# Transposes as pairs of 64-row products, and a first block whose exchanged input is made by copies

## The chip, the core and the metric

The kernel runs on one core of a Trainium2 chip. The metric is the device time of one execution in microseconds (us). The core has a matrix engine (TensorE; in the rows PE for its products and PEld for the loads of their stationary operand), a vector engine (VectorE, DVE), a scalar engine (ScalarE, ACT), GpSimd (POOL) and SyncE (SP), which issues the DMA transfers.

## What is computed

Three stages follow each other, in float32: a convolution whose seven weights per token and head come out of a softmax, and two feed-forward layers.

```python
w = softmax(weight_gen)                        # 2 x 4096 tokens, 8 heads, 7 taps
out[b, s, h] = sum over k of w[b, s, h, k] * x[b, s + k - 6, h]   # x: 2 x 4096 x 192
h = out @ w_in                                 # 192 -> 2048
y = (h * np.cos(h)) @ w_out                    # 2048 -> 192
h2 = y @ w_in2
result = np.maximum(0.01 * h2, h2) @ w_out2
```

## The kernel before

The 8192 tokens are cut into 16 blocks of 512. A block is first convolved with the tokens on the partitions (VectorE, or in parts GpSimd), then turned, so that the 192 channels lie on the partitions and the 512 tokens along them, then taken through the first layer (m = 0) and the second (m = 1), and turned back for the output. A layer is worked in 16 chunks of 128 hidden channels. For accuracy every operand is split into a high and a low float32r part, and a product is made as high x high, high x low and low x high.

**Products as pairs of 64 rows.** The 192 channels are 128 + 64, so products with 128 rows would leave half of the array empty on the rest. All products of the layers have 64 rows (`SIDES` are the lower and the upper 64 partitions), and two of them, one on each side, run in the array at the same time (lines 789 and 799; the rows say `64*128 64x512`). Since a side can only read its own 64 partitions, each block's input stands in three tiles: `x..n` (channels 0 to 127, high and low), `x..s` (the same with its halves exchanged, made by two DMAs in `crossed`, line 473), and `x..r` (the last 64 channels on both sides). An input piece (`hidden`, line 786) is nine products: three with `n`, three with `r`, three with `s`.

**Transposes.** A transpose is a product with the identity. In `attention` (14 blocks) the op `both` makes four of 128 x 128 out of `xa` (line 561) and two out of `xb` (line 566), into the PSUM banks `tm` and `tr`. In `attention_summed` (the two blocks that run first, `LINE[:2]` = 2 and 3) the seven taps are transposed one by one and added in PSUM (line 599). In `take` each finished block of the second layer is turned back in the same way (lines 908 and 912). All of these use 128 rows. In what follows one such group of six in the middle of the products is called a turn: there are 14 of the convolution and 16 of the output. `keep_going` (line 936) are idle transposes that keep the engine running at the start.

**Evacuation.** `turned` copies `tm` to `x0n` high (ACT) and subtracts for the low part (DVE). `place` does the same for the rest, 64 x 256 on each side, and sends the other side's half by one DMA per side; `place_whole` does it without a DMA for the two first blocks. 

**What sets the order.** The function is run once on a plan: each step is an `op` with a due time, a cost for each engine that may do it, what it reads and writes, and its buffers. `Plan.emit` is a list scheduler: it writes the engines' instruction streams from these due times and costs. On the chip each instruction waits by semaphores for what it reads itself; the plan's dependencies only decide where in its engine's stream it stands. `piece` makes the ops of the products and `part` cuts the list of steps into pieces; an input piece there reads all of `n`, `s` and `r` at once (line 804).

Of the kernel before, what the change touches and what calls it, by code (L numbers as in the profile page):

```python
# [14 lines left out]
ALU = mybir.AluOpType  # L15
# [184 lines left out]
def conv_attention_moe_moe(ctx, tc, x, weight_gen, w_in1, w_out1, w_in2, w_out2, out):  # L200
# [27 lines left out]
    SWITCH = 0.43  # L228
# [68 lines left out]

    def minus(e, out, a, b):
        eng[e].tensor_tensor(out=out, in0=a, in1=b.bitcast(F32), op=ALU.subtract)  # L299
# [173 lines left out]
    def crossed(m, b, due):  # L473
        xn, xs, xr = x_of[m, b]
        for j in range(2):
            to, of_ = SIDES[j], SIDES[1 - j]
            op(due, {"SP": 0.8}, lambda e, to=to, of_=of_: nc.sync.dma_start(
                out=xs()[to].bitcast(F32), in_=xn()[of_].bitcast(F32)), [("xhi", m, b), ("xlo", m, b)], [("xs", m, b, j)], [xn, xs])

    def attention(b, begins):  # L480
# [76 lines left out]
        tm, tr = bank(f"tm{b}", ("tq", 2)), bank(f"tr{b}", ("tq", 2))  # L557
# [10 lines left out]
        def both(e):  # L568
            turn(e)
            turn_rest(e)  # L570

        op(last, {"PE": 0.66 + SWITCH}, both, [(k, b, q) for q in kinds for k in ("xam", "xbr")] + ["ident"],
           [("tm", b), ("tr", b)], [xa, xb, tm, tr])
        turned(b, last, tm, tr)

    def attention_summed(b, begins):

        xt, own = xt_of[b]
        ksm, smw, s0 = sm_of[b]
        tm, tr = bank(f"tm{b}", ("tq", 2)), bank(f"tr{b}", ("tq", 2))  # L580
        x_tiles(0, b)
        last = begins - 2
        for i, k in enumerate(reversed(range(K))):
            pr = row(f"pr{b}_{k}")
            reads = [ksm, ("xt", b, 1)]
            if k < HALO and b in LINE[:2]:
                reads.append(("xt", b, 2))
            if k < own:
                reads += [("xt", b, 0, *j) for j in ((0,), (1,), ("z", 0), ("z", 1))]

            def product(e, k=k, pr=pr):
                win = xt().rearrange("p (q h g) -> p q h g", h=H, g=G)[:, k : k + Q]
# [3 lines left out]
            def total(e, to, c, i=i, pr=pr):  # L596
                for q in range(Q):
                    v = pr()[:, q, c]
                    nc.tensor.matmul(  # L599
                        to()[: v.shape[-1], q * P : (q + 1) * P], v, ident, is_transpose=True,  # L600
                        start=i == 0 and q == 0, stop=i == K - 1 and q == Q - 1,
                    )
# [3 lines left out]
            for to, key, c, late in ((tm, "tm", slice(0, P), 0.5), (tr, "tr", slice(P, D), 0.55)):  # L606
                op(due + late, {"PE": 0.44}, lambda e, to=to, c=c, total=total: total(e, to, c),
                   [("pr", b, k), "ident"] + ([(key, b)] if i else []), [(key, b)], [pr, to])
        turned(b, last, tm, tr)

    def turned(b, last, tm, tr):
        xn, xs, xr = x_of[0, b]
        op(last + 0.4, {"ACT": 0.59}, lambda e: copy(e, xn()[:, 0], tm()), [("tm", b)], [("xhi", 0, b)], [xn, tm])
        op(last + 0.8, {"DVE": 0.68}, lambda e: minus(e, xn()[:, 1], tm(), xn()[:, 0]), [("tm", b), ("xhi", 0, b)], [("xlo", 0, b)], [xn, tm])
        crossed(0, b, last + 1)
        if b in SUMMED:
            place_whole(b, last + 0.6, tr)
            return
        place(0, b, last + 1, ("tr", b), tr, lambda: tr()[:, :HT])

    def place_whole(b, due, tr):

        xr = x_of[0, b][2]
        lo, up = SIDES
        op(due, {"ACT": 0.58}, lambda e: copy(e, xr()[lo, 0], tr()[lo]), [("tr", b)], [("rh", 0, b, 0)], [xr, tr])
        op(due + 0.2, {"DVE": 0.68}, lambda e: minus(e, xr()[lo, 1], tr()[lo], xr()[lo, 0]), [("tr", b), ("rh", 0, b, 0)], [("rl", 0, b, 0)], [xr, tr])
        op(due + 0.4, {"ACT": 0.58}, lambda e: copy(e, xr()[up, 0], tr()[lo]), [("tr", b)], [("rh", 0, b, 1)], [xr, tr])
        op(due + 0.6, {"DVE": (0.43,), "ACT": 0.63}, lambda e: copy(e, xr()[up, 1], xr()[lo, 1].bitcast(F32)), [("rl", 0, b, 0)], [("rl", 0, b, 1)], [xr])

    def place(m, b, due, key, src, v):  # L630

        xr = x_of[m, b][2]
        halves = (SIDES[0], slice(0, HT)), (SIDES[1], slice(HT, T))
        for i, (p, c) in enumerate(halves):
            op(due, {"ACT": 0.39}, lambda e, p=p, c=c: copy(e, xr()[p, 0, c], v()[p]), [key], [("rh", m, b, i)], [xr, src])
            op(due + 0.2, {"DVE": 0.42 if m == 0 else (0.41,)}, lambda e, p=p, c=c: minus(e, xr()[p, 1, c], v()[p], xr()[p, 0, c]),
               [key, ("rh", m, b, i)], [("rl", m, b, i)], [xr, src])
            op(due + 0.5, {"SP": 0.4}, lambda e, p=p, p2=SIDES[1 - i], c=c: nc.sync.dma_start(
                out=xr()[p2, :, c].bitcast(F32), in_=xr()[p, :, c].bitcast(F32)), [("rh", m, b, i), ("rl", m, b, i)], [("rx", m, b, i)], [xr])
# [136 lines left out]
    def chunk(pos, st, m, b, f):  # L776
# [27 lines left out]
        reads = [((n, "i", j), "hi", 0), ((n, "i", j), "lo", 0), ("xhi", m, b), ("xlo", m, b)]  # L804
        reads += [k for k in plan.writers if k[0] in ("xs", "rh", "rl", "rx") and k[1:3] == (m, b)]
# [3 lines left out]
        made["in", pos] = hidden, reads, [h, xn, xs, xr], kh  # L809
# [66 lines left out]
    def take(due, st, m, b, am, ar):  # L876
# [9 lines left out]
        halves = (slice(0, R), slice(0, HT), slice(R, P)), (slice(R, P), slice(HT, T), slice(0, R))  # L886
        op(due + 0.1, {"DVE": 0.68, "ACT": 0.58}, lambda e: copy(e, om(), am()), [k], [("om", m, b)], [am, om])
        for i, (p, c, p2) in enumerate(halves):
            op(due, {"ACT": 0.38}, lambda e, p=p, c=c, p2=p2: copy(e, sw()[p], ar()[p2, c]), [k], [("sw", m, b, i)], [ar, sw])
            op(due + 0.2, {"DVE": 0.42}, lambda e, p=p, c=c: nc.vector.tensor_tensor(  # L890
                out=s()[p], in0=ar()[p, c], in1=sw()[p], op=ALU.add), [k, ("sw", m, b, i)], [("s", m, b, i)], [ar, sw, s])
        if m == 0:
# [8 lines left out]
            place(1, b, due + 0.3, k, s, lambda: s())  # L901
            return
        o = row(f"osb{b}", "osb")
        pm, pr = bank(f"pm{b}", ("tq", 2)), bank(f"pr{b}", ("tq", 2))

        def main(e):
            for q in range(Q):
                nc.tensor.transpose(pm()[:, q * P : (q + 1) * P], om()[:, q * P : (q + 1) * P], ident)  # L908

        def rest(e):  # L910
            for j in range(2):
                nc.tensor.transpose(pr()[:, j * P : (j + 1) * P], s()[:, j * P : (j + 1) * P], ident)  # L912

        due += 5
        def both(e):
            main(e)
            rest(e)

        op(due, {"PE": 0.66 + SWITCH}, both, [("om", m, b), ("s", m, b, 0), ("s", m, b, 1)],
           [("pm", b), ("pr", b)], [om, s, pm, pr])  # L920
        op(due + 0.5, {"ACT": 0.59, "DVE": 0.69}, lambda e: copy(e, o()[:, :, :P], pm().rearrange("p (q t) -> p q t", q=Q)),
           [("pm", b)], [("osb", b, 0)], [pm, o])
        op(due + 0.6, {"ACT": 0.38, "DVE": 0.42}, lambda e: copy(
            e, o().rearrange("p (a j) d -> p j a d", a=2)[:, :, :, P:], pr()[:, :HT].rearrange("p (j a d) -> p j a d", j=2, a=2)),
           [("pr", b)], [("osb", b, 1)], [pr, o])
        op(due + 1, {"SP": 1.35}, lambda e: nc.sync.dma_start(out=of[:, Q * b : Q * b + Q, :], in_=o()),
           [("osb", b, 0), ("osb", b, 1)], [("out", b)], [o])
# [23 lines left out]
    def piece(key, nows, due):  # L951
        reads, writes, bufs, then = ["order"], ["order"], [], []
        for side, at in enumerate(key):
# [3 lines left out]
            if at[0] == "in":  # L957
                pos = 2 * at[1] + side
                _, r, bs, kh = made["in", pos]
                reads, bufs = reads + r, bufs + bs  # L960
# [40 lines left out]
    for key, nows in pieces:  # L1001
        dues = []
        for side, at in enumerate(key):
            if at:
                dues.append(2 * at[1] + side + (0 if at[0] == "in" else 2 * LAG + 1 + 0.3 * at[2]))
# [7 lines left out]
    for i in range(IDLE_TURNS):  # L1013
        op(3.0, {"PE": 0.44}, keep_going, [("tm", LINE[0]), ("tr", LINE[0])], (), [spare])
# [29 lines left out]
```

## Time and profile before

| | us |
|---|---|
| median of three runs (1210.36 to 1211.6) | 1211.28 |
| the profiled execution's own time | 1209.89 |
| its span (first to last instruction) | 1208.1 |

| engine | busy, us | share of the span |
|---|---|---|
| PE | 1182.8 | 98% |
| PEld | 1016.0 | 84% |
| DVE | 886.1 | 73% |
| ACT | 847.0 | 70% |
| POOL | 443.0 | 37% |

The span is shorter than the time by what lies around it, 1.79 us. Busy time of PE counts the two sides' products together where they overlap, and the ends of products are modelled; a busy PE is therefore read by the distance between the starts of products, not by its share. The granted clock is that of TensorE, 1.00 being 2.4 GHz and 0.50 being 1.2 GHz.

### The profile page before, as it was taken

The page shows a single profiled execution, that of the slowest core. Times are in us where ns is not written, and L with a number is a line of the kernel's source. Part 1 is how long each engine was busy: PE and PEld are TensorE (multiplying, and loading weights), DVE is VectorE, ACT ScalarE, POOL GpSimd, SP SyncE. Part 2 cuts the span into 40 slices and gives each one's busy share as a digit, 9 for nine tenths or more (in the row PEclk, how much of TensorE's full clock was granted, in tenths as well). Part 3 has the DMA queues.
Part 4 walks back from the last instruction along what each step waited for, and adds up shares of the span by engine and source line. Part 5 has one row for each costly group of instructions (what it writes and reads, how often), then busy time and mean ns, then how long its engine had stood idle before and what let it go on. Part 6 is the DMA issues. An engine that isn't in the chain of part 4 may idle for free.

```text
span 1208.1 us, 25074 instructions
## 1 busy us (share of the span) xinstructions
PE 1182.8 (98%) x10072; PEld 1016.0 (84%) x10072; DVE 886.1 (73%) x1299; ACT 847.0 (70%) x1484; POOL 443.0 (37%) x331
## 2 busy tenths in 40 slices
PE   7998899999999999999999999999999999999998
PEld 6786788888888888888888888888888888888886
DVE  6898887887868687786867768786776868746532
ACT  4898657886766767677676867767676676767753
POOL 4786632670523416052240614325051341504200
PEclk8999899999999999999999999999999999999999
DMA  7534320122120121211012120211212012020100
GB/s 195 162 80 112 106 75 14 40 60 53 47 53 1 47 53 63 53 46 46 10 47 53 47 53 10 77 30 47 53 47 53 1 47 53 14 54 14 28 1 27
DMA packets 30516, 62.69 MB, mean 52 GB/s; under 512 B 3396, under 2 KB 21314, under 8 KB 30400
## 3 DMA queue, kind: packets, MB, share of 16 engines
q1 hardware_dynamic: 30400, 61.08, 18.3%
q8 instruction: 80, 1.31, 0.5%
q14 instruction: 36, 0.29, 0.1%
HBM read 30.13 MB, written 6.29 MB: 30 GB/s over the span
## 4 chain that ended last, share of the span: by engine, by line
PE 92%; DMA 2%; DVE 2%; POOL 1%; issue 1%; ACT 1%; SPq 0%; DVEq 0%; POOLq 0%; ACTq 0%
PE ps L799 46%; PE ps L789 44%; PE ps L908 1%; DMA w01in<-in_moe_w_in 1%; PE ps L561 1%; PE ps L599 1%; DMA x1r<-x1r 1%; DMA xt<-in_x 0%; POOL ilo L299 0%; DMA x0s<-x0n 0%; PE ps L912 0%; DVE lo L299 0%; PE ps L566 0%; DVE g L828 0%; POOL w12in L725 0%
## 5 line engine op out<-in xcount | busy, mean ns | idle before, releaser
L299 POOL TENSOR_TENSOR lo<-g,hi 128x512 fp32r<-128x512 f32 x240 | 335.5, 1399 | 526.1 <-ACT hi L294 480.5
L799 PE MATMUL ps<-hi,ohi 64*128 64x512 f32 x1024 | 403.5, 394 | 0.0
L799 PE MATMUL ps<-hi,olo 64*128 64x512 f32 x1024 | 398.9, 390 | 2.7 <-POOL olo L299 2.7
L799 PE MATMUL ps<-lo,or 64*128 64x512 f32 x1024 | 399.6, 390 | 0.0
L799 PE MATMUL ps<-lo,ohi 64*128 64x512 f32 x1024 | 399.0, 390 | 0.1
L799 PE MATMUL ps<-hi,or 64*128 64x512 f32 x1024 | 398.5, 389 | 0.2 <-POOL or L299 0.2
L299 DVE TENSOR_TENSOR lo<-ps,hi 128x512 fp32r<-128x512 f32 x272 | 186.9, 690 | 162.9 <-ACT hi L294 156.8
L852 ACT ACTIVATE ps<-ps 128x512 f32<-128x512 f32 x256 | 148.8, 582 | 166.6 <-PE ps L789 132.6
L838 DVE TENSOR_TENSOR g<-ps,g 128x512 f32<-128x512 f32 x240 | 165.3, 689 | 86.1 <-ACT g L833 81.9
L799 PEld LDWEIGHTS ps<-hi,olo 64*128 64x128 f32 x1024 | 189.4, 185 | 18.9 <-POOL olo L299 3.1
L799 PEld LDWEIGHTS ps<-lo,ohi 64*128 64x128 f32 x1024 | 189.2, 185 | 16.4 <-DVE lo L299 0.5
L799 PEld LDWEIGHTS ps<-hi,ohi 64*128 64x128 f32 x1024 | 189.4, 185 | 16.1 <-issue 0.2
L799 PEld LDWEIGHTS ps<-lo,or 64*128 64x128 f32 x1024 | 189.5, 185 | 15.0 <-issue 2.4
L789 PE MATMUL ps<-x1n,ihi 64*128 64x512 f32 x512 | 199.6, 390 | 2.5 <-DVE x0n L299 2.5
L799 PEld LDWEIGHTS ps<-hi,or 64*128 64x128 f32 x1024 | 189.6, 185 | 13.4 <-POOL or L299 0.6
L789 PE MATMUL ps<-x0s,ihi 64*128 64x512 f32 x512 | 198.6, 391 | 1.8 <-DMA x0s<-x0n 1.8
L789 PE MATMUL ps<-x1r,ihi 64*128 64x512 f32 x512 | 199.8, 390 | 0.5 <-DMA x1r<-x1r 0.5
L789 PE MATMUL ps<-x1s,ihi 64*128 64x512 f32 x512 | 199.2, 389 | 0.7 <-DMA x1s<-x1n 0.7
L789 PE MATMUL ps<-x0n,ihi 64*128 64x512 f32 x512 | 199.6, 394 | 0.2 <-DVE g L838 0.2
L789 PE MATMUL ps<-x0r,ihi 64*128 64x512 f32 x512 | 198.0, 390 | 0.0
L833 ACT ACTIVATE g<-g 128x512 f32<-128x512 f32 x256 | 161.0, 631 | 45.3 <-DVE g L828 43.1
L828 DVE SCALAR_TENSOR_TENSOR g<-g,ps 128x512 f32<-128x512 int32 x256 | 174.7, 684 | 23.7 <-ACT g L821 18.8
(227 smaller groups left out, 2636.7 us busy)
## 6 DMA issues: line engine op xcount, KB each, us to landing
xt<-in_x SPq DMA_DIRECT2D x12, 960.0 KB, 5.4
x0s<-x0n SPq DMA_DIRECT2D x32, 256.0 KB, 3.8
x1s<-x1n SPq DMA_DIRECT2D x32, 256.0 KB, 3.7
out<-osb SPq DMA_DIRECT2D x16, 384.0 KB, 2.8
x0r<-x0r SPq DMA_DIRECT2D x28, 128.0 KB, 3.8
x1r<-x1r SPq DMA_DIRECT2D x28, 128.0 KB, 3.4
smw<-in_weight_gen SPq DMA_DIRECT2D x3, 448.0 KB, 4.9
xt<-in_x SPq DMA_DIRECT2D x3, 384.0 KB, 4.4
```

Of the source, the lines that this page charges most:

```text
L299: eng[e].tensor_tensor(out=out, in0=a, in1=b.bitcast(F32), op=ALU.subtract)
L561: nc.tensor.transpose(tm()[:, q * P : (q + 1) * P], xa()[:, q, :P], ident)
L599: nc.tensor.matmul(to()[: v.shape[-1], q * P : (q + 1) * P], v, ident, is_transpose=True, start=i == 0 and q == 0, stop=i == K - 1 and q = ...
L789: return nc.tensor.matmul(h(), w[rows, j, d], x()[rows, v], start=i == 0, stop=i == 8)
L799: return nc.tensor.matmul(to(), w[r, f % GF, :], v()[r], start=f == 0 and to_side == 0 and i in (0, 3), stop=f == NF - 1 and to_side == 1 ...
L828: nc.vector.scalar_tensor_tensor(out=g(), in0=g().bitcast(I32), scalar=-2 * math.pi, in1=h(), op0=ALU.mult, op1=ALU.add)
L833: nc.scalar.activation(out=g(), in_=g(), func=AF.Sin, bias=math.pi / 2)
L838: nc.vector.tensor_tensor(out=h() if bank_low else g(), in0=h(), in1=g(), op=ALU.mult)
L852: op(pos + 0.6, {"ACT": 0.58}, lambda e: nc.scalar.activation(out=h(), in_=h(), func=AF.Prelu, alpha=0.01), [kh], [kg], [h])
L908: nc.tensor.transpose(pm()[:, q * P : (q + 1) * P], om()[:, q * P : (q + 1) * P], ident)
```

## The change

Three things, beside the renaming that comes with them (`half`, `side_of`, `rows_of` only name slices).

1. All transposes that carry data become products of 64 rows: `turn64` takes one side's 64 partitions, with a 64 x 64 piece of the identity as the moving operand, and the two sides write two PSUM banks (`tx[0]`, `tx[1]`; `po[0]`, `po[1]` for the output). A turn is then 12 products where there were 6; a tap of a summed block is 16 where there were 8. What is copied out of PSUM is cut by bank, so that four copies of 128 x 256 and of 64 x 128 stand where one of 128 x 512 and one or two of 64 x 256 stood. `place` and `turned` send the second sides' halves in `second` as four DMAs, where there were two. The plan's cost of a turn loses `SWITCH` (0.43).
2. For the first block of the line (`LINE[0]`) `by_copies` makes `x0s` by four copies of 64 x 512 on DVE or ACT in place of two DMAs. The rest of the second summed block goes to its other side by one DMA in place of a copy.
3. In the plan an input piece is split in three (the products with `n`, with `r`, with `s`), and each reads only its own tiles. Seven idle transposes at the start read the new key.

```diff
+    def turn64(out, v, side, **flags):
+        r = SIDES[side]
+        nc.tensor.matmul(out, v, ident[r, r.start : r.stop], is_transpose=True, **{"start": True, "stop": True, **flags})
...
     def part(step):
         kind, p, i = step
-        return (kind, p) if kind == "in" else (kind, p, i // 3 if i < 6 else 2)
+        return kind, p, i // 3 if kind == "in" or i < 6 else 2
...
         def turn(e):
             for q in range(Q):
-                nc.tensor.transpose(tm()[:, q * P : (q + 1) * P], xa()[:, q, :P], ident)
-
-        def turn_rest(e):
+                for i in range(2):
+                    turn64(tx[i]()[:, q * R : (q + 1) * R], xa()[SIDES[i], q, :P], i)
             v = xb().rearrange("p j a r -> p j (a r)")
             for j in range(2):
-                nc.tensor.transpose(tr()[:, j * P : (j + 1) * P], v[:, j], ident)
...
+                for i in range(2):
+                    turn64(tx[i]()[:, HT + j * R : HT + (j + 1) * R], v[SIDES[i], j], i)
...
-        op(due, {"PE": 0.66 + SWITCH}, both, [("om", m, b), ("s", m, b, 0), ("s", m, b, 1)],
+        op(due, {"PE": 0.66}, back, [("om", m, b), ("s", m, b, 0), ("s", m, b, 1)], [("po", b)], [om, s, *po])
...
+        if b == LINE[0]:
+            by_copies(b, last + 0.9)
+        else:
+            crossed(0, b, last + 1)
...
+    def by_copies(b, due):
+        xn, xs, xr = x_of[0, b]
+        for v, k in enumerate(("xhi", "xlo")):
+            for j in range(2):
+                op(due + 0.4 * v, {"DVE": (0.43,), "ACT": 0.63}, lambda e, v=v, j=j: copy(e, xs()[SIDES[j], v], xn()[SIDES[1 - j], v].bitcast(F32)),
+                   [(k, 0, b, 0), (k, 0, b, 1)], [("xs", 0, b, j, v)], [xn, xs])
+
+    def second(m, b, due, keys):
+        xr = x_of[m, b][2]
+        for a, ks in enumerate(keys):
+            for v in range(2):
+                op(due, {"SP": 0.2}, lambda e, a=a, v=v: nc.sync.dma_start(
+                    out=half(xr()[SIDES[1 - a], v], a).bitcast(F32), in_=half(xr()[SIDES[a], v], a).bitcast(F32)),
+                   ks, [("rx", m, b, a, v)], [xr])
...
-        reads = [((n, "i", j), "hi", 0), ((n, "i", j), "lo", 0), ("xhi", m, b), ("xlo", m, b)]
-        reads += [k for k in plan.writers if k[0] in ("xs", "rh", "rl", "rx") and k[1:3] == (m, b)]
+        ws = [((n, "i", j), "hi", 0), ((n, "i", j), "lo", 0)]
+        reads = [
+            ws + [k for k in plan.writers if k[0] in kinds and k[1:3] == (m, b)]
+            for kinds in (("xhi", "xlo"), ("rh", "rl", "rx"), ("xs",))
+        ]
```

**PE at a turn of the convolution in the middle of the program.** `xa` and `xb` are the convolved block, `x1s` and `x1n` inputs of the second layer. Before:

```order
L789 MATMUL ps_370<-x1s_4345,ilo_104 128x512
L799 MATMUL ps_188<-hi_2037,or_102 128x512
L789 MATMUL ps_370<-x1s_4345,ihi_103 128x512
L561 MATMUL ps_341<-ident,xa_4410 128x128 x4
L566 MATMUL ps_181<-ident,xb_4717 128x128 x2
L799 MATMUL ps_188<-lo_2042,or_102 128x512
L799 MATMUL ps_372<-hi_2008,ohi_100 128x512
L789 MATMUL ps_339<-x1n_4323,ihi_108 128x512
```

With the change, where the two rows with `xa` stand four times in turn, and then the two rows with `xb` twice:

```order
L832 MATMUL ps_183<-x1s_4536,ilo_104 128x512
L842 MATMUL ps_164<-hi_2142,or_102 128x512
L832 MATMUL ps_183<-x1s_4536,ihi_103 128x512
L308 MATMUL ps_382<-ident,xa_4567 128x64
L308 MATMUL ps_380<-ident,xa_4567 128x64
...
L308 MATMUL ps_382<-ident,xb_4924 128x64
L308 MATMUL ps_380<-ident,xb_4924 128x64
...
L842 MATMUL ps_164<-lo_2176,or_102 128x512
L842 MATMUL ps_421<-hi_2134,ohi_100 128x512
L832 MATMUL ps_181<-x1n_4508,ihi_108 128x512
```

The place of the turn among the products is the same; six instructions into two banks have become twelve, alternately into one bank and the other.

**ACT where the first block is taken out of PSUM.** `x0n`, `x0r` and `x0s` are its input tiles, the other names are weights. Before:

```order
L719 ACTIVATE w01in<-w01in 128x768
L697 ACTIVATE wt00out<-w00out 128x384
L697 ACTIVATE wt01in<-w01in 128x768
L294 ACTIVATE x0n_284<-ps_181 128x512
L294 ACTIVATE x0r_290<-ps_188 64x512 x2
L719 ACTIVATE w00out<-w00out 128x384
L294 ACTIVATE ihi_83<-wt01in 128x768
```

With the change:

```order
L762 ACTIVATE w01in<-w01in 128x768
L740 ACTIVATE wt00out<-w00out 128x384
L740 ACTIVATE wt01in<-w01in 128x768
L762 ACTIVATE w00out<-w00out 128x384
L293 ACTIVATE x0n_345<-ps_181 128x4x64
L293 ACTIVATE x0n_345<-ps_183 128x4x64
L293 ACTIVATE x0r_362<-ps_181 64x4x64
L293 ACTIVATE x0r_362<-ps_183 64x4x64
L293 ACTIVATE x0s_377<-x0n_345 64x512 x2
L293 ACTIVATE x0r_362<-x0r_362 64x512
```

The copy of `w00out` has moved ahead of the block's, the three copies of the block have become four smaller ones, and three copies between its own tiles follow.

## Rows read from the trace of the kernel before

**Rows 1.** The page: granted clock in 40 slices, and the last chain by engine.

```profile
PEclk8999899999999999999999999999999999999999
...
PE 92%; DMA 2%; DVE 2%; POOL 1%; issue 1%; ACT 1%; SPq 0%; DVEq 0%; POOLq 0%; ACTq 0%
```

**Rows 2.** Stretches: length; PE, PEld, DVE, ACT, POOL busy; clock; DMA; GB/s.

```profile
19.40:43.80 24.40, 22.56 (x142) 16.65 (x141) 22.98 (x35) 17.49 (x32) 15.43 (x16) 0.86 0.44 125
...
196.00:268.00 72.00, 72.00 (x625) 62.34 (x624) 58.47 (x90) 59.40 (x104) 43.11 (x29) 1.00 0.17 48
268.00:1126.00 858.00, 858.00 (x7444) 740.10 (x7442) 633.37 (x924) 606.87 (x1066) 282.53 (x206) 1.00 0.15 41
```

**Rows 3.** PE in order of time, 352 to 357 us: start, length, instruction.

```profile
352.88 0.39 PE L789 MATMUL ps<-x1s,ihi 64*128 64x512 f32 x1
352.89 0.39 PE L799 MATMUL ps<-hi,or 64*128 64x512 f32 x1
353.21 0.66 PE L561 MATMUL ps<-ident,xa 128*128 128x128 f32 x4
...
354.02 0.50 PE L799 MATMUL ps<-lo,or 64*128 64x512 f32 x1
...
354.36 0.40 PE L789 MATMUL ps<-x1n,ihi 64*128 64x512 f32 x1
...
356.90 0.39 PE L789 MATMUL ps<-x1n,ihi 64*128 64x512 f32 x1
```

**Rows 4.** PE in the same order, in two narrower stretches (from 353.60 and 353.70 us).

```profile
353.38 0.49 PE L561 MATMUL ps<-ident,xa 128*128 128x128 f32 x3
...
353.49 0.38 PE L561 MATMUL ps<-ident,xa 128*128 128x128 f32 x2
```

**Rows 5.** Line 561 from 353 to 354 us: shortest, median, longest in ns.

```profile
L561 PEld LDWEIGHTS ps<-ident,xa x4: 140/140/142, 353.2 to 353.5; 128*128 128x128 f32 x4
L561 PE MATMUL ps<-ident,xa x4: 272/273/330, 353.2 to 353.6; 128*128 128x128 f32 x4
```

**Rows 6.** Waits of PEld from 150 us on: us in all, times, longest.

```profile
PEld ps L908 <- issue: 5.5, 15, 0.4
PEld ps L561 <- issue: 4.7, 13, 0.4
...
PEld ps L789 <- issue: 2.5, 15, 0.2
```

**Rows 7.** The chain that ended last, in order of time: start, length, work.

```profile
20.67 3.90 DMA x0s<-x0n
...
43.82 0.69 DVE x0n L299
...
158.29 0.95 DVE xa L514
...
1179.49 0.59 PE ps L908 x4
```

**Rows 8.** Evacuation of one block: ACT and SP's queue in order of time.

```profile
497.48 0.59 ACT L294 ACTIVATE x0n<-ps 128x512 fp32r<-128x512 f32 x1
497.96 0.76 ACT L294 ACTIVATE x0r<-ps 64x256 fp32r<-64x256 f32 x2
...
500.31 1.92 SPq L638 DMA_DIRECT2D x0r<-x0r x2
```

**Rows 9.** Tile x0n from 496 to 530 us: its first use by PEld.

```profile
L789 PEld LDWEIGHTS ps<-x0n,ihi x15: 184/184/185, 514.5 to 529.6; 64*128 64x128 f32 x15
```

**Rows 10.** The page's DMA issues: count, size, median us to landing.

```profile
x0r<-x0r SPq DMA_DIRECT2D x28, 128.0 KB, 3.8
```

**Rows 11.** The start in order of time, 12 to 37 us.

```profile
19.37 0.69 DVE L299 TENSOR_TENSOR x0n<-ps,x0n 128x512 fp32r<-128x512 f32 x1 [3.43 <-ACT x0n L294]
...
21.18 0.42 DVE L296 CAST x0r<-x0r 64x512 fp32r<-64x512 f32 x1
```

**Rows 12.** Waits of PE from 19 to 160 us: us in all, times, longest.

```profile
PE ps L789 <- DMA x0s<-x0n: 1.8, 2, 1.3
```

More of the change, by code (lines that the diff above doesn't have):

```diff
@@ L477, in crossed @@
             op(due, {"SP": 0.8}, lambda e, to=to, of_=of_: nc.sync.dma_start(
-                out=xs()[to].bitcast(F32), in_=xn()[of_].bitcast(F32)), [("xhi", m, b), ("xlo", m, b)], [("xs", m, b, j)], [xn, xs])
+                out=xs()[to].bitcast(F32), in_=xn()[of_].bitcast(F32)), [k for k in plan.writers if k[0] in ("xhi", "xlo") and k[1:3] == (m, b)], [("xs", m, b, j)], [xn, xs])
     def attention(b, begins):
@@ L594, in product, with total @@
                 eng[e].tensor_tensor(out=pr().rearrange("p q (h g) -> p q h g", h=H), in0=win, in1=wgt, op=ALU.mult)
[L596 to L602, printed above, removed]
+            def total(e, i=i, pr=pr):
+                parts = [(0, slice(0, P)), (HT, slice(P, D))]
+                for at, c in reversed(parts) if i == K - 1 else parts:
+                    for q in range(Q):
+                        for side in range(2):
+                            v = pr()[SIDES[side], q, c]
+                            turn64(
+                                tx[side]()[: v.shape[-1], at + q * R : at + (q + 1) * R], v, side,
+                                start=i == 0 and q == 0 and not at, stop=i == K - 1 and q == Q - 1 and not at,
+                            )
@@ L630, in place @@
-    def place(m, b, due, key, src, v):
-        xr = x_of[m, b][2]
[L633 to L639, printed above, removed]
+            op(due + 0.5, {"PE": 0.88}, total, [("pr", b, k), "ident"] + ([("tx", b)] if i else []), [("tx", b)], [pr, *tx])
@@ new lines, in place @@
+    def place(m, b, due, key, s):
+        xr = x_of[m, b][2]
+        for a, p in enumerate(SIDES):
+            op(due, {"ACT": 0.39}, lambda e, p=p, a=a: copy(e, half(xr()[p, 0], a), s()[p]), [key], [("rh", m, b, a)], [xr, s])
+            op(due + 0.2, {"DVE": (0.41,)}, lambda e, p=p, a=a: minus(e, half(xr()[p, 1], a), s()[p], half(xr()[p, 0], a)),
+               [key, ("rh", m, b, a)], [("rl", m, b, a)], [xr, s])
+        second(m, b, due + 0.5, [[("rh", m, b, a), ("rl", m, b, a)] for a in range(2)])
@@ L885, in take @@
         k = ("acc", m, b)
-        halves = (slice(0, R), slice(0, HT), slice(R, P)), (slice(R, P), slice(HT, T), slice(0, R))
         op(due + 0.1, {"DVE": 0.68, "ACT": 0.58}, lambda e: copy(e, om(), am()), [k], [("om", m, b)], [am, om])
[L888 to L891, printed above, removed]
+        for i, p in enumerate(SIDES):
+            op(due, {"ACT": 0.38}, lambda e, p=p, i=i: copy(e, sw()[p], half(ar()[SIDES[1 - i]], i)), [k], [("sw", m, b, i)], [ar, sw])
+            op(due + 0.2, {"DVE": 0.42}, lambda e, p=p, i=i: nc.vector.tensor_tensor(
+                out=s()[p], in0=half(ar()[p], i), in1=sw()[p], op=ALU.add), [k, ("sw", m, b, i)], [("s", m, b, i)], [ar, sw, s])
         if m == 0:
@@ L900, in take, with back @@
             plan.writers[k] = plan.writers["s", m, b, 0] + plan.writers["s", m, b, 1]
-            place(1, b, due + 0.3, k, s, lambda: s())
+            place(1, b, due + 0.3, k, s)
             return
         o = row(f"osb{b}", "osb")
-        pm, pr = bank(f"pm{b}", ("tq", 2)), bank(f"pr{b}", ("tq", 2))
-        def main(e):
+        po = [bank(f"po{b}{i}", ("tq", 2)) for i in range(2)]
+        def back(e):
             for q in range(Q):
-                nc.tensor.transpose(pm()[:, q * P : (q + 1) * P], om()[:, q * P : (q + 1) * P], ident)
@@ L910, in rest @@
-        def rest(e):
+                for i in range(2):
+                    turn64(po[i]()[:, q * R : (q + 1) * R], om()[SIDES[i], q * P : (q + 1) * P], i)
             for j in range(2):
-                nc.tensor.transpose(pr()[:, j * P : (j + 1) * P], s()[:, j * P : (j + 1) * P], ident)
+                for i in range(2):
+                    turn64(po[i]()[:, HT + j * R : HT + (j + 1) * R], s()[SIDES[i], j * P : (j + 1) * P], i)
         due += 5
-        def both(e):
-            main(e)
-            rest(e)
@@ new lines, in take @@
+        for i in range(2):
+            op(due + 0.5, {"ACT": 0.39, "DVE": 0.42}, lambda e, i=i: copy(
+                e, o()[:, :, i * R : (i + 1) * R], po[i]()[:, :HT].rearrange("p (q d) -> p q d", q=Q)),
+               [("po", b)], [("osb", b, 0, i)], [po[i], o])
+            op(due + 0.6, {"ACT": 0.28, "DVE": 0.31}, lambda e, i=i: copy(
+                e, o()[:, 2 * i : 2 * i + 2, P:], po[i]()[:, HT : HT + P].rearrange("p (q d) -> p q d", q=2)),
+               [("po", b)], [("osb", b, 1, i)], [po[i], o])
```

85 lines of the change are left out of this document (47 added, 38 removed).

## The prediction, on record before the result

> **What bounds the kernel now.** I read the page first, for the engine that the end hangs on: the last chain runs through PE for 92% of the span, and the clock digits are 9 almost throughout [rows 1]. Then the stretches, to see where PE is not alone: from 196 us on PE is busy for the whole of each stretch while DVE and ACT are busy for 58 and 59 of 72 us; from 19.4 to 43.8 us DVE is busy for 22.98 of 24.4 us and the clock is 0.86 on average [rows 2]. So after the start a microsecond taken from PE is a microsecond of the time, and in the start it need not be. Then PE in order of time around one turn, which is what the change rewrites [rows 3 to 5], and the waits of PEld, to see how many turns look alike [rows 6]. In the chain in order of time the turns are pieces of PE's own work [rows 7].
>
> **What a turn costs today.** In steady work the pairs start every 0.23 us: from 354.36 to 356.90 are eleven of them [rows 3]. The last pair before the turn starts at 352.88, the second one after it at 354.36. That is 1.48 us for two pairs, so the turn costs 1.48 - 0.46 = 1.02 us. Its six transposes start 0.11 us apart, at 353.38 and 353.49 for instance [rows 4], and take 0.65 us. The other 0.37 us is the passage from 64 rows to 128 and back: PE starts nothing between 352.89 and 353.21, and the loads of the first instruction on either side stand open. How long such a load is shows in the first product after a pause, which is longer by it: a transpose 330 against 272 ns, so 0.06 us [rows 5]; a product of 64 rows 0.50 against 0.39 or 0.40, so 0.11 us [rows 3]. The wait "issue" of PEld ahead of a turn is there 15 times for the output and 13 times for the convolution, each about 0.37 us, and 0.17 us behind it [rows 6]. So 28 of the 30 turns lie where PE sets the pace; one of the convolution precedes a wait in the start, where the chain goes on through DVE at 158 us [rows 7], and one of the output is in the tail. I count these two at nothing.
>
> **What a turn will cost.** Twelve products of 64 rows, six on either side, with 64 moving columns where there were 128. Two things are taken as given by rows: the two sides run at the same time, as the products do, which start in pairs [rows 3]; and no change of rows is left, so the 0.37 us goes. What the trace does not show is how far apart such pairs start. From below: half the columns in half of 0.11 us, 0.055 us. A load must be done before each, and the two nearest rows differ: 0.06 us for a transpose of 128 rows, 0.11 us for a product of 64 rows. From above, a side that loads and streams one after the other: 0.11 + 0.055 = 0.165 us, at which the turn would cost 0.94 us and gain 0.08. I take 0.07 us: the load belongs to the operation (same float32 data, same mode, same 128 columns), to which the row at 0.06 us is nearest, and 0.01 us is added since 64-row pairs are not seen to run without a margin. The load of the product behind the turn, 0.11 us, is covered by the last pair only in part. So a turn costs 5 x 0.07 + 0.11 = 0.46 us and saves 1.02 - 0.46 = 0.56 us; 28 turns save 15.7 us.
>
> The Trainium skill, "TensorE: Matmul & The Clock Gate", section "LDWEIGHTS (loading the stationary operand)", speaks against this choice: a load takes its columns divided by 1.2 GHz whatever its rows, 107 ns for 128 columns. The trace agrees for the products and not for the 128-row transposes. By it a turn would save 0.36 us and the sum would be that of the first rival.
>
> **Copies out of PSUM and DMAs.** A block now has one copy of 0.59 us and two in 0.76 us on ACT, and as many subtractions on DVE [rows 8]; with the change six of each, of about 0.4 us for 256 columns and somewhat less for 128: some 0.5 us more on each engine per block, and less for the output. In 72 us with 13 us free on each engine [rows 2] that is covered. The two more DMAs per block and layer take SP about 1 us each (1.92 us for two) [rows 8]. The last DMA of this block is issued by 502.2 us, and its input is first read at 514.5 [rows 9]; a landing takes 3.8 us [rows 10], so more than 6 us stay free. If that cover went, a late block would stop PE for each microsecond beyond it; I price it at nothing.
>
> **The start.** The products with `x0s` wait 1.8 us for two DMAs of 3.9 us [rows 7, 12], and the mean clock of 0.86 means up to 0.14 x 24.4 = 3.4 us of lost speed in that stretch [rows 2]. If the copies take both away and nothing else holds, 5.2 us are gained. But DVE is busy for all but 1.4 us of that stretch, and it makes the products of the second block, for which PE waits next. DVE's stream gets 1.5 us longer: four instructions of 0.42 us and three copies of 0.42 for the first block in place of one of 0.69, one as long and one copy [rows 11], and four in place of two for the second. ACT gets about as much, and now copies a weight ahead of the block. Splitting the input pieces changes where they stand in PE's stream and nothing that they wait for. The 56 tap transposes and their passages of the second block cost PE less too, in the same stretch, where DVE makes the taps. So the bounds are 5.2 us gained and 1.5 us lost; I take 0, because the engine that is late next is the one that gets more to do.
>
> **The sum.** It is made against the profiled execution: 1209.89 - 15.7 = 1194.2 us (span 1192.4). That execution lies 1.39 us under the median of the runs shown, so the forecast for a median is 1195.6 us. About 0.2%, 2.4 us, is what a measurement of this kernel can tell from no change.
>
> **Rivals.**
> 1. The load is that of 64 rows. Pairs start every 0.11 us, a turn costs 5 x 0.11 + 0.11 = 0.66 us, 28 turns save 10.1 us: 1201.2 us. For it: the only loads of 64 x 128 in the trace are the products', and a row that covers half of the partitions may simply load more slowly. Against: those products are of another kind (float32r), and their data need not be loaded as a transpose's are.
> 2. The passage stays. If what empties the array is not the number of rows but the kind of product, the 0.37 us stays at 0.46 + 0.37 = 0.83 us a turn, saving 5.3 us: 1206.0 us. For it: every turn of today changes both at once. Against: nothing in the rows names the kind.
> 3. The two sides do not overlap for such short products, slower than before. Each of the twelve then costs what each of the six costs now, 0.11 us [rows 4]: 1.31 us a turn, 0.29 us more than today, 28 turns 8.1 us more: 1219.4 us. It decides from the point at which a product of 64 columns costs more than 0.085 us (1.02 / 12). For it: twice as many instructions, and no row with so short a product. Against: within a pair the products start 0.01 us apart [rows 3].
> 4. The start gains or loses what rows bound, or a late DMA stops PE: 5.2 us less or up to 1.5 us more on top of any of these.
>
> To rival 3 the Trainium skill, same page, section "Back-to-back issue gap", has a milder form: with hardware decoding off, each product takes 62 ns to issue. No row here shows it; by it twelve take 0.74 us and a turn would save 0.28 us.
>
> **How the numbers follow.** The forecast has a chance of 0.50, rival 1 of 0.26, rival 2 of 0.13, rival 3 of 0.07; 0.04 is left for a start or a wait that takes everything back. The low end is a pair every 0.06 us (5 x 0.06 + 0.11 = 0.41, saving 17.1 us) with the full gain of the start, 22.3 us less: 1189. The high end takes in rival 1 with a start that loses 1.5 us, 1202.7, and rival 2 as it stands: 1206. Left out are rival 3 and the rest, and the far sides of rival 2. Faster: 0.50 + 0.26 + 0.13 = 0.89; within 0.2%: 0.04; slower: 0.07.
>
> **What would show it.** In the changed profile the line of `turn64` should stand in PE's timeline with pairs 0.07 us apart, with no "issue" wait of PEld ahead of it or behind it, and two pairs around a turn 0.92 us apart instead of 1.48. Pairs 0.11 us apart mean rival 1; a gap ahead of or behind the pairs, rival 2; single starts 0.11 us apart, rival 3. The start is right if `x0n` of the second block is subtracted within 1.5 us of 43.8 us [rows 7], and wrong if PE comes out of the first 160 us by some microseconds earlier. Any wait of PE for `x0r` or `x1r` after 200 us would make the part on DMAs wrong.

## The result: 1.2% faster, the turns as forecast, the start not

The changed kernel takes 1196.88 us (median of 4 runs, 1196.44 to 1197.41) against 1210.87 us (4 runs, 1210.36 to 1211.6) for the kernel before: a ratio of 0.9884 [0.9867, 0.9901]. The forecast was 1195.6 us in a range of 1189 to 1206.

### The profile after

The span is 1194.6 us, 13.5 us shorter. The page's clock digits and last chain, which answer to [rows 1]:

```profile
PEclk8899899999999999999999999999999999999999
...
PE 90%; DVE 3%; DMA 2%; POOL 1%; ACT 1%; issue 1%; SPq 0%; ACTq 0%; DVEq 0%; POOLq 0%
```

The same stretches as in [rows 2]:

```profile
19.40:43.80 24.40, 19.29 (x213) 15.72 (x213) 23.71 (x38) 19.38 (x39) 15.72 (x16) 0.86 0.33 96
196.00:268.00 72.00, 71.98 (x654) 62.67 (x652) 57.16 (x89) 61.72 (x116) 42.68 (x29) 1.00 0.16 48
268.00:1126.00 858.00, 858.00 (x7712) 789.19 (x7710) 644.87 (x984) 618.25 (x1134) 285.42 (x207) 1.00 0.15 41
```

PE still fills the whole of the steady stretches, and ACT and DVE have room as before. In the start PE has less to do, DVE a little more, and the clock is no higher.

PE in order of time around one turn, which answers to [rows 3, 4] (start, length, instruction):

```profile
493.25 0.39 PE L842 MATMUL ps<-hi,or 64*128 64x512 f32 x1
493.25 0.39 PE L832 MATMUL ps<-x1s,ihi 64*128 64x512 f32 x1
493.49 0.41 PE L308 MATMUL ps<-ident,xa 64*128 64x64 f32 x8
493.73 0.29 PE L308 MATMUL ps<-ident,xb 64*128 64x64 f32 x4
493.83 0.47 PE L842 MATMUL ps<-lo,or 64*128 64x512 f32 x1
493.83 0.47 PE L842 MATMUL ps<-hi,ohi 64*128 64x512 f32 x1
494.14 0.39 PE L832 MATMUL ps<-x1n,ihi 64*128 64x512 f32 x1
494.15 0.38 PE L842 MATMUL ps<-hi,olo 64*128 64x512 f32 x1
```

The four pairs with `xa` begin at 493.49 and those with `xb` at 493.73: 0.24 / 4 = 0.06 us a pair. The last pair of products before the turn begins at 493.25 and the second one after it at 494.15, 0.90 us where there were 1.48; less two pairs of 0.23 the turn costs 0.44 us. The first product behind it is 0.47 instead of 0.39 us long, which is what is left of its load. The waits of PEld from 150 us on, which answer to [rows 6], no longer name "issue" at a turn; these are the first two, of which the first stands at 163.7 us, behind the convolution's turn that precedes a wait in the start:

```profile
PEld ps L832 <- DVE x0r L311: 2.6, 1, 2.6
PEld ps L308 <- DVE s L935: 1.4, 2, 1.0
```

And all that PE waits for from 200 us on, which stands at the very end, at the last output turn:

```profile
PE ps L308 <- DVE s L935: 1.1, 2, 0.9
```

No wait for `x0r` or `x1r` is left there, so the two more DMAs per block and layer are covered. They land in 3.0 us (the page's DMA issues, [rows 10] before):

```profile
x0r<-x0r SPq DMA_DIRECT2D x56, 64.0 KB, 3.0
```

**Where the time went.** The first output turn (line 908 before, `om` of line 308 after) is a mark that every version has at the same place of the work. Before it lies the start, behind it the steady part with 28 turns, up to the last output turn. The rows of its operand `om`: durations in ns, first and last start in us. Before:

```profile
L908 PE MATMUL ps<-ident,om x64: 272/273/328, 196.9 to 1202.4; 128*128 128x128 f32 x64
```

After:

```profile
L308 PE MATMUL ps<-ident,om x128: 213/222/272, 199.0 to 1188.4; 64*128 64x64 f32 x128
```

The steady part went from 1202.4 - 196.9 = 1005.5 to 1188.4 - 199.0 = 989.4 us: 16.1 us, 0.575 us a turn. The start lost 2.1 us. What lies behind the mark at the end went from 5.7 to 6.2 us: the four copies of the last output turn all follow its products now, where the large one ran ahead of the last two products before. So -16.1 + 2.1 + 0.5 = -13.5 us.

**Where the start lost it.** Not in the stretch that the prediction watches. The second block's `x0n` is subtracted at 43.67 us (DVE in order of time), as before [rows 7]:

```profile
43.67 0.76 DVE L311 TENSOR_TENSOR x0n<-ps,x0n 128x256 fp32r<-128x256 f32 x2
```

The wait for `x0s` of the first block [rows 12] is gone; instead PE waits, at 51.3 us, for the DMA that replaced a copy in the second block's rest:

```profile
PE ps L832 <- DMA x0r<-x0r: 1.8, 1, 1.8
```

PE falls behind for good between 110 and 145 us, where the weights of the second layer are split into high and low parts by ACT, DVE and POOL, one group of four chunks after another. PE's waits there, in the changed kernel:

```profile
PE ps L832 <- POOL ilo L311: 3.9, 1, 3.9
PE ps L842 <- POOL olo L311: 3.1, 1, 3.1
...
```

and before, where the two are hardly shorter:

```profile
PE ps L789 <- POOL ilo L299: 3.7, 1, 3.7
PE ps L799 <- POOL olo L299: 2.7, 1, 2.7
```

So it is not their length that counts but when they end.

POOL makes the low part `ilo` of `w12in`, the third group's input weights. POOL in order of time before:

```profile
125.35 2.46 POOL L725 TENSOR_TENSOR w12in<-wt12in,w12in 128x768 int32<-128x768 int32 x1 [2.07 <-DVE wt12in L711]
...
130.90 2.56 POOL L299 TENSOR_TENSOR ilo<-w12in,ihi 128x768 fp32r<-128x768 f32 x1
```

and after:

```profile
127.57 2.46 POOL L768 TENSOR_TENSOR w12in<-wt12in,w12in 128x768 int32<-128x768 int32 x1 [2.07 <-DVE wt12in L754]
...
133.12 2.56 POOL L311 TENSOR_TENSOR ilo<-w12in,ihi 128x768 fp32r<-128x768 f32 x1
```

It ends at 133.46 before and at 135.68 after, 2.2 us later, and the first output turn comes 2.1 us later. That the one makes the other was a guess at this point; the experiments below test it.

Where these 2.2 us come from can be followed in the two traces. The chain that ended last passes, in both, through the low part of `x1r`, the second layer's first input. POOL made it before, and with the change the plan gives it to DVE. Before:

```profile
101.29 1.31 POOL x1r L299
```

After:

```profile
103.53 1.28 DVE x1r L311
```

Two steps of a softmax (`smm`) stand beside it in DVE's stream, and DVE comes out of the three 2.4 us later than before (106.28 against 103.91 us at the same instruction). From there to 137 us DVE works through the same instructions in the same order in both kernels, and `wt12in`, for which POOL's `w12in` waits, begins at 126.48 instead of 124.26 us. On the way the lag falls to 0.6 us at 113.7 us, where DVE had waited for PE before, and comes back in `wt10out`, 2.65 us long instead of 1.28: in both kernels it ends 0.8 us behind POOL's `ilo` of `w11in`, which is itself 2.2 us late. The second profile of the change has the same three there. No run moves them back, so this is read from traces and not tested, and `x1r` alone doesn't decide it: DVE makes it in experiment 7 too, with `ilo` ready at 133.27 us, and POOL in experiment 6, with `ilo` at 139.25.

Behind the wait the clock differs too: the granted clock of 110 to 145 us is 0.85 on average (0.90 before), and the chain goes on in products 0.42 us apart instead of 0.23, at the lower level of 1.2 GHz. Before, that lasted to 136.3 us, seven pairs; now it lasts to 141.9 us, fourteen:

```profile
135.73 0.79 PE ps L832
136.53 0.42 PE ps L832
136.95 0.42 PE ps L832
```

### The profile page after: what moved, and what is told of

Same layout as the page of the kernel before. It is cut to its first block, busy times and chain, and to the rows that moved or that the text cites. A ratio compares the mean times of both kernels' runs of the same rounds, so it can differ in the third digit from the quotient of the medians.

```text
span 1194.6 us, 25907 instructions
## 1 busy us (share of the span) xinstructions
PE 1161.4 (97%) x10364; PEld 1049.5 (88%) x10364; DVE 892.5 (75%) x1356; ACT 852.4 (71%) x1554; POOL 440.3 (37%) x330
## 4 chain that ended last, share of the span: by engine, by line
PE 90%; DVE 3%; DMA 2%; POOL 1%; ACT 1%; issue 1%; SPq 0%; ACTq 0%; DVEq 0%; POOLq 0%
PE ps L842 47%; PE ps L832 41%; PE ps L308 1%; DMA w00out<-in_moe_w_out 1%; DMA w00in<-in_moe_w_in 0%; DVE lo L311 0%; DMA w03in<-in_moe_w_in 0%; POOL ilo L311 0%; DMA x1r<-x1r 0%; ACT hi L293 0%; DVE g L874 0%; ACT g L879 0%; SPq L699 0%; DVE wt00out L754 0%; DVE wt10out L754 0%
```

## The experiments

All of them in one table. "Steady" is from the first output turn to the last, "`ilo` ready" is the end of POOL's `ilo<-w12in`; both are from one profile of each, and the runs of one version lie 0.6 to 5.4 us apart. A ratio is to the kernel before on the same chip. Experiments 1 to 4 share a chip, 5 to 8 a second, 9 to 11 a third, and 12 has a fourth: between these groups the ratios are what can be compared.

| version | median us | ratio | `ilo` ready | first output turn | steady |
|---|---|---|---|---|---|
| before | 1210.87 | | 133.46 | 196.9 | 1005.5 |
| the change | 1196.88 | 0.9884 [0.9867, 0.9901] | 135.68 | 199.0 | 989.4 |
| 1 neither copies nor split | 1204.16 | 0.9955 [0.9942, 0.9968] | 141.64 | 206.1 | 989.4 |
| 2 turns in 128 rows | 1213.46 | 1.0030 [1.0018, 1.0042] | 137.70 | 201.6 | 1005.5 |
| 3 one side ahead of the other | 1199.10 | 0.9913 [0.9898, 0.9928] | 137.05 | 200.7 | 991.8 |
| 4 an idle 128-row transpose | 1207.71 | 0.9983 [0.9973, 0.9992] | 137.89 | 202.2 | 1000.1 |
| 5 old start | 1195.32 | 0.9889 [0.9874, 0.9904] | 134.48 | 198.2 | 989.5 |
| 6 copies, no split | 1199.97 | 0.9927 [0.9912, 0.9941] | 139.25 | 202.4 | 989.5 |
| 7 split, no copies | 1194.13 | 0.9876 [0.9860, 0.9893] | 133.27 | 197.0 | 989.5 |
| 8 the change again | 1197.93 | 0.9910 [0.9895, 0.9925] | 136.09 | 199.6 | 989.5 |
| 9 old start, split | 1198.00 | 0.9901 [0.9886, 0.9916] | 137.85 | 201.6 | 989.5 |
| 10 as 7, a copy for a DMA | 1193.00 | 0.9862 [0.9846, 0.9879] | 132.49 | 195.8 | 989.5 |
| 11 as 7, again | 1195.17 | 0.9881 [0.9865, 0.9896] | 134.20 | 197.9 | 989.5 |
| 12 second layer's weights due earlier | 1188.93 | 0.9825 [0.9812, 0.9839] | 120.36 | 193.0 | 989.4 |

### The turn: experiments 2, 3 and 4

**2. Turns in 128 rows.** The taps, the copies and the split as changed; `attention` and `take` transpose in 128 rows again.

```diff
-                for i in range(2):
-                    turn64(tx[i]()[:, q * R : (q + 1) * R], xa()[SIDES[i], q, :P], i)
+                nc.tensor.transpose(tm()[:, q * P : (q + 1) * P], xa()[:, q, :P], ident)
```

> The change without its turns: the 14 turns of the convolution and the 16 of the output are made in 128 rows and evacuated as before; the taps of the two first blocks, the copies and the split pieces stay. Theory (turns save 16.4 us, the rest of the change costs 2 to 4 us): 1213 to 1215 us, the product number 900 at 158 us or later, 1.02 us a turn. Rival (the start costs nothing by itself): 1210.9 us within 0.2%.

Steady is again that of before, 1005.5 us, and the waits of PEld at the turns are back:

```profile
PEld ps L963 <- issue: 5.5, 15, 0.4
PEld ps L573 <- issue: 4.7, 13, 0.4
```

So all of the 16 us is in the turns and what is copied out of them, and the rest of the change by itself makes the kernel slower, by 0.3%: the first output turn comes 4.7 us later than before.

**3. One side ahead of the other.** The six products of one side stand ahead of the six of the other, in the convolution's turns and in the output's.

```diff
-            for q in range(Q):
-                for i in range(2):
+            for i in range(2):
+                for q in range(Q):
                     turn64(tx[i]()[:, q * R : (q + 1) * R], xa()[SIDES[i], q, :P], i)
```

> The change, but in each turn the six products of one side stand in PE's stream ahead of the six of the other, where they alternate in the change. If the two sides overlap only because the stream alternates, the starts are 12 in a row at 0.0625 us: a turn costs 0.43 + 6 x 0.0625 = 0.81 us, 28 turns 10.5 us more than the change, about 1207 us. If each side runs on its own whatever the order in the stream, a turn stays at 0.43 us and the time at about 1197 us.

PE in order of time:

```profile
495.43 0.46 PE L308 MATMUL ps<-ident,xa 64*128 64x64 f32 x6
495.68 0.22 PE L308 MATMUL ps<-ident,xb 64*128 64x64 f32 x1
495.73 0.22 PE L308 MATMUL ps<-ident,xa 64*128 64x64 f32 x1
495.74 0.22 PE L308 MATMUL ps<-ident,xb 64*128 64x64 f32 x1
495.77 0.47 PE L841 MATMUL ps<-lo,or 64*128 64x512 f32 x1
495.79 0.22 PE L308 MATMUL ps<-ident,xa 64*128 64x64 f32 x1
495.85 0.28 PE L308 MATMUL ps<-ident,xb 64*128 64x64 f32 x2
495.95 0.47 PE L841 MATMUL ps<-hi,ohi 64*128 64x512 f32 x1
```

Although all six of one side stand first in the stream, the other side's `xa` run among them (495.73, between two `xb` of the first side), and one side takes up its next product (495.77) while the other still transposes (495.79, 495.85). The steady part is 2.4 us longer, at most 0.09 us a turn: the sides go side by side whatever their order, and rival 3 has no ground.

**4. An idle 128-row transpose behind each turn.** The same line stands behind the output's turn, into `po[1]`.

```diff
+            nc.tensor.transpose(tx[1]()[:, HT + P :][:, :P], ident, ident)
```

> The change with one idle 128-row transpose of the identity behind each turn, into a free part of the second bank. If the passage of 0.37 us belongs to the change of rows, a turn costs 0.43 + 0.11 + 0.37 = 0.91 us, 28 turns 13.4 us more than the change: about 1210 us. If it had another cause (the kind of product, or six instructions from another place), only the 0.11 us is added: about 1200 us.

```profile
499.68 0.39 PE L843 MATMUL ps<-hi,or 64*128 64x512 f32 x1
499.88 0.42 PE L308 MATMUL ps<-ident,xa 64*128 64x64 f32 x8
500.13 0.30 PE L308 MATMUL ps<-ident,xb 64*128 64x64 f32 x4
500.36 0.33 PE L579 MATMUL ps<-ident 128*128 128x128 f32 x1
500.62 0.50 PE L843 MATMUL ps<-lo,or 64*128 64x512 f32 x1
...
500.96 0.39 PE L843 MATMUL ps<-hi,olo 64*128 64x512 f32 x1
```

From 499.68 to 500.96 are 1.28 us, against 0.90; over the steady part it is (1000.1 - 989.4) / 28 = 0.38 us a turn. The transpose itself is 0.11 [rows 4], so some 0.27 us are the passage to 128 rows and back: it belongs to the change of rows, since the transposes of 64 rows, products of the same kind, have none, and rival 2 falls. It is less than the 0.37 us that I read before, and the profile lists no "issue" wait of PEld for it.

### The start: experiments 1 and 5 to 11

**1. Neither copies nor split pieces**, all transposes in 64 rows.

```diff
-        if b == LINE[0]:
-            by_copies(b, last + 0.9)
-        else:
-            crossed(0, b, last + 1)
+        crossed(0, b, last + 1)
...
-        return kind, p, i // 3 if kind == "in" or i < 6 else 2
+        return (kind, p) if kind == "in" else (kind, p, i // 3 if i < 6 else 2)
```

> All transposes in 64 rows as in the change, but the first block's x0s by DMAs as before, and an input piece reads n, r and s at once as before. Theory: a turn costs 0.43 us in place of 1.02, 28 of them save 16.4 us, and what the changed kernel lost up to its 900th product (2.2 to 3.8 us) comes from the copies of the first block and the split pieces. Then the time is about 1210.9 - 16.4 = 1194.5 us and the product number 900 starts within 1 us of 156.1 us. Rival: the loss of the start belongs to the 64-row transposes and their evacuation (more and smaller copies, a DMA for the second block). Then the time stays at about 1197 us and the product number 900 starts 2 us or more late.

Without the two parts that I suspected of the start's loss it lost more: the first output turn comes 9.2 us later than before. My first theory fell, and the rival's 1197 us is passed too. POOL in order of time shows the same two instructions, later still:

```profile
135.58 4.13 POOL L765 TENSOR_TENSOR w12in<-wt12in,w12in 128x768 int32<-128x768 int32 x1
139.79 1.85 POOL L311 TENSOR_TENSOR ilo<-w12in,ihi 128x768 fp32r<-128x768 f32 x1
```

**5. The old start** (128-row taps, whole copies, DMAs, unsplit pieces), 64-row turns elsewhere: the start's functions as before the change, `turn64` only in `attention` and `take`.

> The turns of attention and of the output as 64-row products; the two summed blocks, their evacuation, the DMAs of x0s and the unsplit input pieces as before. Theory (the start's loss comes with the 64-row taps, their evacuation in smaller pieces and the order that the plan then gives): the start is that of before, product 900 begins within 1 us of before's 156.1 us, 28 turns save 0.585 us each, 16.4 us: about 1193.8 us, under both kernels. Rival (the start loses whatever is done there, because the plan shifts the weights' preparation as soon as turns cost less): product 900 begins 2 us or more later than before's and the time is that of the changed kernel, 1196 to 1198 us.

Product 900 (the products of the layers are counted in order of start) begins 1.3 us later than before's, between the two expectations, and 1195.32 us lies between them too. Against the change itself (experiment 8, same chip) it is 2.6 us faster.

**6 and 7. Copies without the split; the split without copies.** They are the two halves of the edit of experiment 1.

> The changed kernel with input pieces unsplit in the plan (an input piece reads n, r and s at once), copies for x0s kept. The start with neither copies nor split pieces lost 9.4 us at product 900, the changed kernel's loses 2.2 to 3.9. Theory: the split only changes where pieces stand in PE's stream and is worth less than 2 us: 1197 to 1199 us. Rival: the split gives back most of the 6 us, because products with n can then go ahead of the exchanged tiles: about 1202 us.

> The changed kernel with x0s of the first block made by two DMAs again, split pieces kept. Theory: the copies give back most of the 6 us that the start without both loses more: about 1201 to 1203 us. Rival: with split pieces the DMAs are covered by the products with n and r, and the time stays at 1196 to 1198 us.

Experiment 6 lies between its two expectations: beside the copies the split is worth 2.0 us (1199.97 against 1197.93 us of experiment 8, no runs in common), near the theory's bound and far from the rival's 6 us. In 7 the theory fell and the time is under the rival's too: beside the split the copies cost 3.8 us (1197.93 against 1194.13 us, no runs in common). Yet against experiment 1, made on another chip, either part by itself gains: the split 10.0 us (ratio 0.9955 to 0.9876), the copies 4.2 us (0.9955 to 0.9927). What one part is worth depends on the other.

**8. The change once more.**

> The changed kernel once more, on the same chip as the three others, to compare with them: 1196 to 1198 us, product 900 2 to 4 us later than before's.

As expected: 1197.93 us, and the start 2.7 us later than before's.

**9. The old start with split pieces**: experiment 5 with the change's edit of `part` and of what a piece reads.

> The start of before (128-row taps, whole copies, DMAs for x0s) with the 64-row turns of the rest, and input pieces split in three. Theory (without copies the split lets products with n and r go ahead of the exchanged tiles, and it is the copies that cost DVE its time): product 900 begins within 1 us of before's 156.1 us or earlier, 1192 to 1195 us. Rival (any new order that the plan gives to the weights of the second layer costs 2 us or more in this start): 1196 to 1199 us.

1198.00 us and product 900 4.7 us later than before's: the theory fell, and the rival's forecast holds. The split gains nothing here, where with 64-row taps and no copies it had gained 10.0 us. Whether it costs something isn't shown: 1198.00 stands against 1195.32 us of experiment 5 on another chip, with runs that overlap and ratios of 0.9901 [0.9886, 0.9916] and 0.9889 [0.9874, 0.9904]. None of the parts has a price of its own.

**10. As 7, with a copy in place of the DMA for the second block's rest.**

```diff
-        if b == LINE[0]:
+        if b in SUMMED:
             for v in range(2):
                 op(last + 1, {"DVE": (0.43,), "ACT": 0.63}, lambda e, v=v: copy(...
```

> The changed kernel without the copies for x0s, and the second summed block's rest again by a copy in place of a DMA. Theory: the DMA is covered by split pieces, so the copy can only load DVE or ACT: the time of the version without the copies for x0s, 1193 to 1195 us, or up to 1 us more. Rival: the DMA is one of the waits that hold the second block (1.8 us for x0r in the changed kernel's profile), and the copy gives 1 to 2 us: about 1192.5 us.

1193.00 us is the low end of the theory's range; against experiment 11 on the same chip it is 2.2 us less, which is nearer to the rival's gain. Its runs (1192.82 to 1193.65) touch those of experiment 11, 1193.61 to 1197.55, so that the copy gains is likely and no more.

**11. Experiment 7 again.**

> The changed kernel without the copies for x0s once more, with more rounds: 1193 to 1195 us, a ratio to before of 0.987 to 0.988; if its first time was luck of the start, 1196 us or more.

1195.17 us, just above the range, with one run of 1197.55 us among those of the change; its ratio of 0.9881 can't be told from the change's first, 0.9884, and lies under its second, 0.9910. So that the copies cost something beside the split is shown on one chip (7 against 8) and is likely beyond it.

### What sets the end of the start: experiment 12

The table orders itself by one column. In the first thirteen rows `ilo` of `w12in` is ready between 132.5 and 141.6 us, and the first output turn follows 63.2 to 64.5 us behind it, in whatever way taps, copies and pieces were arranged. So what each part did to the start shows in the time at which these weights are ready. To test whether the weights hold the start back I left taps, copies and split as changed and made the weights of the second layer, all four groups, due 6 us earlier:

```diff
-                due = need[m, g * GF] + WDUE[i]
+                due = need[m, g * GF] + WDUE[i] - 6 * m
```

> The changed kernel with one edit: the plan's due times of the second layer's weights are 6 us earlier (m = 1 alone). Theory (the start ends with these weights: in ten profiles product 1000 begins 39 to 40.5 us after POOL ends ilo from w12in, which in the changed kernel ends at 135.7 us against 133.5 before): ilo from w12in ends earlier than 133.5 us, product 1000 begins 39 to 40.5 us behind it unless another wait takes over, and the time is 1190 to 1195 us, under the changed kernel's 1196.9 to 1197.9. Rival (the weights' end only marks the lag that taps and copies made before): whatever order POOL has, product 1000 begins 2 us or more later than before's 172.75 us, and the time stays at 1196 us or more.

POOL in order of time:

```profile
116.31 2.11 POOL L768 TENSOR_TENSOR w12in<-wt12in,w12in 128x768 int32<-128x768 int32 x1 [1.43 <-DVE wt12in L754]
118.50 1.86 POOL L311 TENSOR_TENSOR ilo<-w12in,ihi 128x768 fp32r<-128x768 f32 x1
```

PE's waits from 110 to 145 us:

```profile
PE ps L832 <- DVE x1r L311: 2.7, 1, 2.7
PE ps L832 <- DVE lo L311: 1.5, 1, 1.5
...
```

`ilo` is ready 15.3 us earlier than in the change, PE's waits for POOL's weights are gone from this stretch, and the start ends 6.0 us earlier, at 193.0 us. The rest of the 15.3 is not gained, since other waits take over: `x1r`, the second layer's input, 2.7 us to 113.2 us, and last `lo`, the low part of a hidden chunk, 1.5 us to 131.0 us; the first output turn now follows 72.6 us behind `ilo`. With 1188.93 us and a ratio of 0.9825 [0.9812, 0.9839] this version beats the change, by its ratio, and the kernel before. The rival falls. What is shown is that the due times of the second layer's weights hold back the end of the start in the change; that it is `w12in` among them rests on the table and on the chain, which goes from POOL's `ilo` to PE, and the edit moves other work in the streams too. It wasn't combined with experiment 10, and other shifts than 6 us weren't run.

## Why the prediction was right, and where it wasn't

- **What bounds, and the 28 turns: right.** The steady part holds all of the gain, and its length is the same, 989.4 to 989.5 us, in every version whose turns are those of the change.
- **The turn's cost: right in mechanism, close in size.** 0.46 us was forecast, 0.44 us measured; 15.7 us saved against 16.1. The pair is 0.06 us apart, not 0.07: the margin of 0.01 that I added isn't there. A load of 0.11 us before each, rival 1, is excluded. Whether a load of 0.06 us [rows 5] or the 64 moving columns (0.055 us, from below) sets the pace of the pairs, no run tells apart, since both give 0.06.
- The Trainium skill, "TensorE: Matmul & The Clock Gate", section "LDWEIGHTS (loading the stationary operand)", has a load take its columns divided by 1.2 GHz, by which an estimate for 128 columns is 107 ns. The trace disagrees for these loads: pairs with 128 stationary columns begin 0.06 us apart. The same page of the Trainium skill, section "Back-to-back issue gap", gives 62 ns to each product with hardware decoding off. Here twelve begin within 0.34 us, so they aren't issued at that pace.
- **The passage: right.** No "issue" wait is left at the turns, and experiment 4 brings a passage back with the 128 rows, 0.27 us of the 0.37.
- **Copies out of PSUM and DMAs: right.** PE waits for none of the blocks' inputs after 200 us. Only at the end, which I put at nothing, the smaller copies cost 0.5 us.
- **The start: wrong.** I took 0 and bounded it by 1.5 us lost; it lost 2.1 and 2.7 us in two profiles. The step that failed is that "the engine that is late next" was sought only in the stretch that the diff touches, 19 to 44 us. There it held: the wait for `x0s` went, the clock stayed at 0.86, and `x0n` passed my test at 43.8 us. But the plan writes all streams from due times, and the time was lost from 103 us on: DVE fell 2.4 us behind with work that the plan had moved there, and POOL's `ilo`, for which PE waits, came 2.2 us later. The waits for `ilo` and `olo` stood in the profile of before. For being wrong I had named only that PE comes out of the first 160 us earlier; it came out later. A second sentence failed beside it: "Splitting the input pieces changes where they stand in PE's stream and nothing that they wait for". The split was worth 10.0 us without the copies, 2.0 us beside them, and nothing that can be shown in the old start.
- **Luck.** That the start came out within 3 us of the 0 that I took is luck: my reason for 0 didn't decide it, and the versions of the table begin their steady part from 3.9 us earlier to 9.2 us later than before.
- **The sum.** The forecast for the profiled execution's span was 1192.4 us, the span is 1194.6: 0.4 us more saved by the turns, 2.1 us lost in the start, 0.5 at the end.

## What to carry to other kernels

Count a repeated stall from two marks around it, price its replacement by the nearest row of the same kind of operation, and let the rest of the sum be small. Where a scheduler writes the streams, an edit need not have a local price: compare every engine's order as far as the next long wait, and take the end of that wait, not the edited place, as the mark. When many variants scatter, plot them against one instruction's end; here that led to an edit of one due time worth about 8 us (a ratio of 0.9825 against 0.9884 and 0.9910).

## What the runs showed of the hardware that I had not expected

- Two 64-row sides don't keep to the order of the stream between them. With six products of one side ahead of six of the other, the second side starts within the first one's work, and a product of the first side starts ahead of transposes of the second that stand before it in the stream (experiment 3: 495.77 ahead of 495.79 and 495.85). The sides' first products behind the turn start 0.18 us apart (495.77 and 495.95), where they start together when the stream alternates (493.83 twice).
- A single 128-row transpose among 64-row work costs 0.38 us, though its own step is 0.11 us (experiment 4).
- What remains open: which instruction ahead of `w12in` pushes DVE and POOL back wasn't isolated by a run in any version, only that the due times of these weights undo it; for the change the traces point to `x1r` and the two softmax steps in DVE's stream. Starts of one version differ by 0.6 to 0.9 us between profiles (the change: 199.0 and 199.6; experiment 7: 197.0 and 197.9), so differences of a microsecond between the starts of the table aren't shown.
